# Feed-forward products in two halves of the TensorE array, in a kernel of routed attention and a bilinear feed-forward block

## The chip, the cores and the metric

The kernel runs on one core of a Trainium2 chip. The metric is the time on the device in microseconds, from one launch. Every engine works from a queue of its own: TensorE (PE, matmuls; its weight loads are shown apart as PEld), VectorE (DVE), ScalarE (ACT), GpSimd (POOL) and SyncE (SP), which starts transfers.

## The reference

There are two blocks. The first is attention with routing: queries and keys of each head are assigned to the nearest of 16 centroids, and a query sees only keys of its own cluster. The second is a feed-forward block whose hidden layer is the product of two linear maps. Everything is fp32 outside the kernel.

```python
# q, k, v: (4 batches, 8 heads, 768 tokens, 64); centroids: (8, 16, 64)
q_assign = argmax(q_n @ c_n.T); k_assign = argmax(k_n @ c_n.T)
mask = q_assign[..., :, None] == k_assign[..., None, :]
scores = where(mask, q @ k.T / 8, -1e9)
attn = softmax(scores) @ v                      # (4, 8, 768, 64)
x = attn.transpose(0, 2, 1, 3).reshape(3072, 512)
# w_a, w_b: (512, 1536); w_out: (1536, 512)
out = ((x @ w_a) * (x @ w_b)) @ w_out           # (3072, 512)
```

## The kernel before

The program goes through 96 groups of attention work. In a group, TensorE makes the scores of two tiles of keys (`score`), the weighted values of the two tiles before (`weigh`), sometimes the denominators of the softmax (`denominators`), and then takes feed-forward pieces of an earlier batch from a queue, as many as a budget of matmul columns allows. When the groups are done, the pieces that are left run one after the other.

The scores of two heads of 64 features stand side by side in the rows of the array: each matmul has 64 rows and 128 columns of weights.

```python
def add(Ts, start):                              # in score()
    for u, s in zip(us, tiles):
        p, hf, j = where(u)
        for a in range(2):
            r = slice(a * D, (a + 1) * D)        # D = 64
            nc.tensor.matmul(
                out=s[:, a, 0:HB],               # HB = 384
                lhsT=Ts[p][r, S + j * P:S + (j + 1) * P],
                rhs=Ts[p][r, hf * HB:(hf + 1) * HB],
                start=start, stop=not start)
```

The weighted values of the two heads, and the denominators likewise, stand side by side in its columns: each matmul has 128 rows and 64 columns of weights, and its output is one half of the partitions of a PSUM tile.

```python
for a in range(2):                               # in weigh()
    nc.tensor.matmul(out=O_of[0][a * D:(a + 1) * D, 0:HB],
                     lhsT=vs[p][:, a, j, :], rhs=probs[u][:, a, :],
                     start=(j == 0), stop=(j == NJ - 1))
# ... and in denominators(), for each term t
for a in range(2):
    nc.tensor.matmul(out=ps[a * D:(a + 1) * D, 0:HB], lhsT=ones,
                     rhs=t[:, a, :], ...)
```

The feed-forward products take the whole array, 128 rows and 128 columns of weights. The first batch has the plain form (`up`), the other three split each product of matrices into seven smaller ones in the manner of Strassen (`product`, once for the two maps up, once for the map down; the map down has this form in all batches).

```python
def up(w_sb, f):                                 # 384 columns, 4 in a sum
    ps = ps_m.tile([P, 512], FP32, name="m")
    for ch in range(NCH):
        nc.tensor.matmul(out=ps[:, 0:HB],
                         lhsT=w_sb[:, ch, f * P:(f + 1) * P],
                         rhs=xTs[b][:, ch, t0:t0 + HB],
                         start=(ch == 0), stop=(ch == NCH - 1))
    return ps
# ...
def product(l, r):                               # up: 384 columns, 2 in a sum
    ps = ps_m.tile([P, 512], FP32, name="m")
    rhs = X[r] if r in X else W[r]
    for c in range(2):
        nc.tensor.matmul(out=ps[:, 0:HB], lhsT=A[l][c], rhs=rhs[c],
                         start=(c == 0), stop=(c == 1))
    return ps[:, 0:HB]
# ...
def product(l, r):                               # down: 256 columns, 6 in a sum
    ps = ps_m.tile([P, 512], FP32, name="m")
    for f in range(N2):
        nc.tensor.matmul(out=ps[:, 0:HN], lhsT=A[l][f // 3][:, f % 3, :],
                         rhs=B[r][f // 2][:, f % 2, :],
                         start=(f == 0), stop=(f == N2 - 1))
    return ps[:, 0:HN]
```

VectorE adds a product that is done into one or two tiles in SBUF, and forms the sums and differences of weights and inputs that the next products take. Three PSUM tiles `m` are shared by all these users. The order within one group of the loop:

```python
score(now)
# ...
weigh(before)
ready[l]()               # for some groups: assignments of the next heads (32-column matmuls, L358)
# ...
denominators(*divmod(g // 3 - 1, 2))             # every third group
# ...
while len(ffn) > least and credit > 0:
    cost, piece = ffn.popleft()
    credit -= cost
    piece()
```

Of the kernel before, what the change touches and what calls it, by code (L numbers as in the profile page):

```python
# [30 lines left out]
P = 128  # L31
# [105 lines left out]
def short_path(nc, tc, ctx, c, cn, centroids_in, casts, n_far, q, k, v,  # L137
# [3 lines left out]
    B, H, S, D = q.shape  # L141
# [5 lines left out]
    NCH = DM // P  # L147
    NF = DF // P
    HB = S // 2
# [36 lines left out]
    def by_blocks(p):  # L186
        return p >= HP
# [332 lines left out]
    probs, accs, O_of, den_of, xTs = {}, {}, {}, {}, {}  # L520
# [125 lines left out]

    ffn = deque()

    def store(b, j, half, y):
        order = "(j p) (half n) -> p j half n" if by_blocks(b * HP) else \  # L650
            "(p j) (half n) -> p j half n"
        rows = out[b * S:(b + 1) * S, :].rearrange(order, j=NJ, half=2)
        nc.sync.dma_start(out=rows[:, j, half, :], in_=y)

    def ffn_block(b, blk):

        box = {}
        t0 = blk * HB

        def up(w_sb, f):  # L660
            ps = ps_m.tile([P, 512], FP32, name="m")
            for ch in range(NCH):
                nc.tensor.matmul(out=ps[:, 0:HB],  # L663
                                 lhsT=w_sb[:, ch, f * P:(f + 1) * P],
                                 rhs=xTs[b][:, ch, t0:t0 + HB],
                                 start=(ch == 0), stop=(ch == NCH - 1))
            return ps

        def piece_a(f):
            if f == 0:  # L670
                box["h"] = hp_.tile([P, NF, HB], FP32, name="h")
            ps = up(wa_sb, f)
            box["a"] = hap.tile([P, HB], FP32, name="ha")
            nc.scalar.copy(out=box["a"], in_=ps[:, 0:HB])

        def piece_b(f):
            ps = up(wb_sb, f)
            nc.vector.tensor_tensor(out=box["h"][:, f, :], in0=box["a"],
                                    in1=ps[:, 0:HB], op=ALU.mult)

        ups = [(NCH * HB, lambda f=f, piece=piece: piece(f))
               for f in range(NF) for piece in (piece_a, piece_b)]
        return ups, box
# [41 lines left out]
    def ffn_ups(b, h):  # L725

        x = xTs[b]
        X = {"11": [x[:, c, 0:HB] for c in (0, 1)],
             "T1": [x[:, c, HB:S] for c in (0, 1)],
             "21": [x[:, c, 0:HB] for c in (2, 3)],  # L730
             "22": [x[:, c, HB:S] for c in (2, 3)]}

        def combine_t4():
            for c in range(2):
                nc.vector.tensor_tensor(out=W["T4"][c], in0=W["T2"][c],
                                        in1=X["21"][c], op=ALU.subtract)

        def products(w_sb, i, is_a):
            N2 = NF // 2
            A = {m + n: [w_sb[:, c, f * P:(f + 1) * P] for c in cs]  # L740
                 for m, f in (("1", i), ("2", i + N2))
                 for n, cs in (("1", (0, 1)), ("2", (2, 3)))}
            box = {}

            def combine(name, l, r, op):

                at = {"S1": 1, "S2": 2, "S3": 0, "S4": 3}[name]
                dst = W["slots"][at]
                for c in range(2):
                    nc.vector.tensor_tensor(out=dst[c], in0=l[c], in1=r[c], op=op)  # L750
                A[name] = dst

            def half_1():
                combine("S1", A["21"], A["22"], ALU.add)
                combine("S2", A["S1"], A["11"], ALU.subtract)

            def half_2():
                combine("S3", A["11"], A["21"], ALU.subtract)
                combine("S4", A["12"], A["S2"], ALU.subtract)
                s = W["slots"]  # L760
                W["slots"] = [s[1], s[2], s[0], s[3]]

            def product(l, r):
                ps = ps_m.tile([P, 512], FP32, name="m")
                rhs = X[r] if r in X else W[r]
                for c in range(2):
                    nc.tensor.matmul(out=ps[:, 0:HB], lhsT=A[l][c], rhs=rhs[c],  # L767
                                     start=(c == 0), stop=(c == 1))
                return ps[:, 0:HB]

            def place(k, f):
                if is_a:
                    return h[k][:, f, :]
                return hap.tile([P, HB], FP32, name="ha")

            def add(out, in0, ps, op=ALU.add):
                nc.vector.tensor_tensor(out=out, in0=in0, in1=ps, op=op)  # L777

            def done(name, k, f):
                if not is_a:  # L780
                    to = h[k][:, f, :]
                    nc.gpsimd.tensor_tensor(out=to, in0=to, in1=box[name],  # L782
                                            op=ALU.mult)

            def p1():
                if not h:
                    h.extend(hp_.tile([P, NF, HB], FP32, name="h")
                             for _ in range(2))
                ps = product("11", "11")
                box["11"] = place(0, i)  # L790
                nc.scalar.copy(out=box["11"], in_=ps)

            def p6():
                ps = product("S2", "T2")
                box["12"] = place(1, i)
                add(box["12"], box["11"], ps)

            def p2_ahead():
                box["P2"] = product("12", "21")

            def p2():
                ps = box.pop("P2") if "P2" in box else product("12", "21")
                add(box["11"], box["11"], ps)
                done("11", 0, i)

            def p7():
                ps = product("S3", "T3")
                box["22"] = place(1, i + N2)
                add(box["22"], box["12"], ps)

            def p4():
                ps = product("22", "T4")
                box["21"] = place(0, i + N2)
                add(box["21"], box["22"], ps, ALU.subtract)
                done("21", 0, i + N2)

            def p5():
                ps = product("S1", "T1")
                add(box["12"], box["12"], ps)
                add(box["22"], box["22"], ps)  # L820
                done("22", 1, i + N2)

            def p3():
                add(box["12"], box["12"], product("S4", "22"))
                done("12", 1, i)

            return half_1, half_2, p2_ahead, [p1, p6, p2, p7, p4, p5, p3]

        parts = [products(w_sb, i, w_sb is wa_sb) for i in range(NF // 2)
                 for w_sb in (wa_sb, wb_sb)]  # L830
        pieces = []
        for n, (half_1, half_2, p2_ahead, ps) in enumerate(parts):
            ps[0] = both(*([half_1] if n == 0 else []), half_2, ps[0])
            if n == 0:
                ps[1] = both(p2_ahead, ps[1])
                ps[2] = both(combine_t4, ps[2])
            if n + 1 < len(parts):
                ps[4] = both(ps[4], parts[n + 1][0])
            pieces += [(2 * HB, f) for f in ps]
        return pieces  # L840
# [9 lines left out]
    def ffn_downs(b, h):  # L850
        N2, HN = NF // 2, DM // 2
        B = {m + n: [wo_sb[:, f + i:f + i + 2, c:c + HN] for i in (0, 2, 4)]
             for m, f in (("1", 0), ("2", N2)) for n, c in (("1", 0), ("2", HN))}
# [16 lines left out]
        def tile_of(n):  # L870
            t = slice(n * P, (n + 1) * P)
            A, C = {}, {}
# [17 lines left out]
            def product(l, r):  # L890
                ps = ps_m.tile([P, 512], FP32, name="m")
                for f in range(N2):
                    nc.tensor.matmul(out=ps[:, 0:HN], lhsT=A[l][f // 3][:, f % 3, :],  # L893
                                     rhs=B[r][f // 2][:, f % 2, :],
                                     start=(f == 0), stop=(f == N2 - 1))
                return ps[:, 0:HN]

            def add(out, in0, ps, op=ALU.add):
# [11 lines left out]
            def p2():  # L910
                add(C["11"], C["11"], product("12", "21"))
                store(b, n, 0, C["11"])
                if n == 1:
                    combine("S4", A["12"], "12", "S2")
# [21 lines left out]
            def p4():  # L936
                add(C["21"], C["21"], product("22", "T4"), ALU.subtract)
                store(b, 3 + n, 0, C["21"])
# [27 lines left out]
    def both(*fs):  # L966
        return lambda: [f() for f in fs]
# [72 lines left out]
    for g in range(NG + 3):  # L1040
        p, l = divmod(g, GPP)
# [59 lines left out]
    def some_ffn(n):  # L1101
        for _ in range(n):
# [15 lines left out]
    ps = ps_m.tile([P, 512], FP32, name="m")  # L1118
    nc.tensor.matmul(out=ps[0:1, 0:1], lhsT=far_off, rhs=ones[:, 0:1],
                     start=True, stop=True)  # L1120
# [227 lines left out]
```

## Time and profile before

| | before |
|---|---|
| time, median of 3 runs | 1064.39 us (1064.03 to 1064.41) |
| span of the profiled run | 1062.4 us |
| TensorE busy | 1049.4 us, 4756 matmul records |
| weight loads | 605.4 us |
| VectorE, ScalarE, GpSimd busy | 708.0, 260.0, 354.3 us |
| granted TensorE clock, mean | 0.999 |

A line of a group in the page has the line of the kernel (L767), the engine, the operation, the tiles written and read, the shape of the operands (for a matmul the rows and columns of the weights, then the moving operand), the number of records, then the busy time and the mean of one in ns, and last the idle time of the engine before them with what ended it. L539 are the scores, L580 the weighted values, L603 the denominators, L358 the assignments; L663, L767 and L893 are the three kinds of feed-forward product in the order above. In the timeline the first column is the start in us from the beginning of the span, the second the time from the start of the first to the end of the last of the records that were merged. One fp32 matmul of the program appears as two records; records of TensorE overlap one another.

### The profile page before, as it was taken

To read this page: it belongs to the slowest core of one execution; us is meant where nothing else is said; L and a number is where in the kernel's file an instruction comes from. 1 tells how busy PE (TensorE), PEld (TensorE's weight loads), DVE (VectorE), ACT (ScalarE), POOL (GpSimd) and SP (SyncE) were. 2 spreads that over 40 slices of the span, in tenths; PEclk is the share of its full clock that TensorE was granted. 3 is DMA by queue.
4 is the path that set the end of the run, shared out by engine and by line. 5 is a ranking of instruction groups with operands and counts; after the bars stand their busy time and mean duration, and the time that the engine had idled before them with its cause. 6 is when DMAs were issued, how large, how long until landed. Compare 5 with 4: busy or idle time off the path is not lost.

```text
span 1062.4 us, 13065 instructions
## 1 busy us (share of the span) xinstructions
PE 1049.4 (99%) x4756; PEld 605.4 (57%) x4756; DVE 708.0 (67%) x1402; ACT 260.0 (24%) x501; POOL 354.3 (33%) x329
## 2 busy tenths in 40 slices
PE   8999999999999999999999999999999999999997
PEld 5444455554557665455445766555545687555686
DVE  6778877887857447676757736767565846676762
ACT  5665333233322221222222121122121200000000
POOL 1111345454533322443545422444334310222200
PEclk9999999999999999999999999999999999999999
DMA  6334253525130120202020030200000000000001
GB/s 173 92 71 99 84 105 104 124 76 131 62 47 20 39 41 22 38 4 45 5 45 1 25 65 24 46 0 20 0 4 1 11 30 21 0 1 1 0 31 33
DMA packets 120504, 46.18 MB, mean 43 GB/s; under 512 B 106608, under 2 KB 115824, under 8 KB 120432
## 3 DMA queue, kind: packets, MB, share of 16 engines
q1 hardware_dynamic: 120016, 44.85, 18.1%
q8 instruction: 39, 0.64, 0.3%
q10 hardware_dynamic: 416, 0.43, 0.1%
q14 instruction: 33, 0.27, 0.1%
HBM read 37.78 MB, written 6.29 MB: 41 GB/s over the span
## 4 chain that ended last, share of the span: by engine, by line
PE 93%; DVE 5%; issue 1%; POOL 1%; DMA 0%; ACT 0%; DVEq 0%; POOLq 0%
PE m L767 30%; PE m L893 20%; PE s L539 14%; PE O L580 12%; PE m L663 11%; PE m L603 2%; PE m L358 1%; DVE raw L723 1%; PE m L342 0%; DVE raw L750 0%; DVE acc L569 0%; DVE xT L723 0%; POOL xT L635 0%; DVE ha L777 0%; DMA wo_sb<-in_centroids_dram 0%
## 5 line engine op out<-in xcount | busy, mean ns | idle before, releaser
L548 ACT ACTIVATE pt<-s 128x768 f32<-128x768 f32 x192 | 145.4, 808 | 307.4 <-PE s L539 253.8
L569 POOL TENSOR_TENSOR acc<-acc,pt 128x384 f32<-128x384 f32 x144 | 151.9, 1068 | 59.8 <-ACT pt L548 43.5
L782 POOL TENSOR_TENSOR h<-h,ha 128x384 f32<-128x384 f32 x72 | 72.6, 1016 | 235.9 <-DVE ha L777 234.4
L580 PE MATMUL O<-pt,v 128*64 128x384 f32 x768 | 145.1, 499 | 0.0
L539 PE MATMUL s<-qkT 64*128 64x384 f32 x768 | 139.6, 483 | 0.0
L777 DVE TENSOR_TENSOR ha<-ha,m 128x384 f32<-128x384 f32 x126 | 66.9, 546 | 74.1 <-PE m L767 73.3
L777 DVE TENSOR_TENSOR h<-h,m 128x384 f32<-128x384 f32 x126 | 67.3, 549 | 64.3 <-PE m L767 63.5
L569 DVE TENSOR_TENSOR acc<-acc,pt 128x384 f32<-128x384 f32 x96 | 73.7, 794 | 35.9 <-POOL acc L569 35.0
L580 PEld LDWEIGHTS O<-pt,v 128*64 128x64 f32 x768 | 46.6, 136 | 86.4 <-issue 84.8
L539 PEld LDWEIGHTS s<-qkT 64*128 64x128 f32 x768 | 70.5, 187 | 31.4 <-issue 0.2
L893 PE MATMUL m<-wo_sb,h 128*128 128x256 f32 x384 | 87.5, 382 | 0.0
L635 POOL TENSOR_TENSOR xT<-xT,acc 128x384 f32<-128x384 f32 x32 | 32.9, 1029 | 147.9 <-DVE acc L630 121.3
L893 PEld LDWEIGHTS m<-wo_sb,h 128*128 128x128 f32 x384 | 72.1, 190 | 16.0 <-issue 4.2
L767 PE MATMUL m<-raw 128*128 128x384 f32 x192 | 70.4, 489 | 0.9 <-DVE ha L777 0.9
L663 PE MATMUL m<-xT,wa_sb 128*128 128x384 f32 x192 | 67.4, 493 | 0.7 <-POOL xT L635 0.7
L663 PE MATMUL m<-xT,wb_sb 128*128 128x384 f32 x192 | 66.8, 491 | 0.0
L893 PE MATMUL m<-xT,h 128*128 128x256 f32 x288 | 65.4, 382 | 0.1
L893 PEld LDWEIGHTS m<-xT,h 128*128 128x128 f32 x288 | 54.1, 190 | 11.7 <-issue 1.7
L767 PE MATMUL m<-xT,wa_sb 128*128 128x384 f32 x144 | 52.9, 491 | 0.4 <-DVE rest L899 0.4
L767 PE MATMUL m<-xT,size 128*128 128x384 f32 x144 | 52.8, 490 | 0.0
L767 PE MATMUL m<-xT,wb_sb 128*128 128x384 f32 x144 | 52.8, 490 | 0.0
L663 PEld LDWEIGHTS m<-xT,wa_sb 128*128 128x128 f32 x192 | 35.4, 190 | 30.5 <-ACT pt L548 3.6
(164 smaller groups left out, 1444.6 us busy)
## 6 DMA issues: line engine op xcount, KB each, us to landing
raw<-in_moe_w_a_dram SPq DMA_DIRECT2D x12, 512.0 KB, 4.4
raw<-in_moe_w_b_dram SPq DMA_DIRECT2D x12, 512.0 KB, 3.7
raw<-in_moe_w_out_dram SPq DMA_DIRECT2D x12, 512.0 KB, 3.3
qk<-in_q_dram SPq DMA_DIRECT2D x48, 96.0 KB, 3.1
qk<-in_k_dram SPq DMA_DIRECT2D x48, 96.0 KB, 3.6
v<-in_v_dram SPq DMA_DIRECT2D x24, 192.0 KB, 3.9
out_dram<-rest SPq DMA_DIRECT2D x24, 128.0 KB, 1.7
v<-in_v_dram SPq DMA_DIRECT2D x4, 384.0 KB, 4.6
```

What stands on the lines that cost most here:

```text
L358: nc.tensor.matmul(out=ps[32 * kq:32 * kq + 32, 0:HB], lhsT=cTb[:, hp, :], rhs=qkTs[p][:, kq * HB:(kq + 1) * HB], start=True, stop=True)
L539: nc.tensor.matmul(out=s[:, a, 0:HB], lhsT=Ts[p][r, S + j * P:S + (j + 1) * P], rhs=Ts[p][r, hf * HB:(hf + 1) * HB], start=start, stop=not ...
L548: nc.scalar.activation(out=pt, in_=s[:, :, 0:HB], func=AF.Exp, scale=SCALE)
L569: eng.tensor_tensor(out=acc[:, a, :], in0=probs[u - 1][:, a, :] if j == 1 else acc[:, a, :], in1=probs[u][:, a, :], op=ALU.add)
L580: nc.tensor.matmul(out=O_of[0][a * D:(a + 1) * D, 0:HB], lhsT=vs[p][:, a, j, :], rhs=probs[u][:, a, :], start=(j == 0), stop=(j == NJ - 1))
L603: nc.tensor.matmul(out=ps[a * D:(a + 1) * D, 0:HB], lhsT=ones, rhs=t[:, a, :], start=(n == 0), stop=(n == len(terms) - 1))
L635: nc.gpsimd.tensor_tensor(out=x, in0=x, in1=den, op=ALU.mult)
L663: nc.tensor.matmul(out=ps[:, 0:HB], lhsT=w_sb[:, ch, f * P:(f + 1) * P], rhs=xTs[b][:, ch, t0:t0 + HB], start=(ch == 0), stop=(ch == NCH - 1))
L767: nc.tensor.matmul(out=ps[:, 0:HB], lhsT=A[l][c], rhs=rhs[c], start=(c == 0), stop=(c == 1))
L777: nc.vector.tensor_tensor(out=out, in0=in0, in1=ps, op=op)
L782: nc.gpsimd.tensor_tensor(out=to, in0=to, in1=box[name], op=ALU.mult)
L893: nc.tensor.matmul(out=ps[:, 0:HN], lhsT=A[l][f // 3][:, f % 3, :], rhs=B[r][f // 2][:, f % 2, :], start=(f == 0), stop=(f == N2 - 1))
```

## The change

Each feed-forward product is made of two matmuls with 64 columns of weights, one in each half of the array's columns, with the same moving operand; their outputs are the two halves of the partitions of the same PSUM tile. The scores, the weighted values, the denominators and all work of the other engines stay as they are. It is meant to give the products the same division of the array as the weighted values and the denominators, which run just before them in a group, so that the array need not change its division between the two.

```diff
+    def in_halves(ps, lhsT, rhs, start, stop):
+        for a in range(2):
+            half = slice(a * D, (a + 1) * D)
+            nc.tensor.matmul(out=ps[half], lhsT=lhsT[:, half], rhs=rhs,
+                             start=start, stop=stop)
 # ... in up()
-                nc.tensor.matmul(out=ps[:, 0:HB],
-                                 lhsT=w_sb[:, ch, f * P:(f + 1) * P],
-                                 rhs=xTs[b][:, ch, t0:t0 + HB],
-                                 start=(ch == 0), stop=(ch == NCH - 1))
+                in_halves(ps[:, 0:HB], w_sb[:, ch, f * P:(f + 1) * P],
+                          xTs[b][:, ch, t0:t0 + HB],
+                          start=(ch == 0), stop=(ch == NCH - 1))
 # ... in product(), up
-                    nc.tensor.matmul(out=ps[:, 0:HB], lhsT=A[l][c], rhs=rhs[c],
-                                     start=(c == 0), stop=(c == 1))
+                    in_halves(ps[:, 0:HB], A[l][c], rhs[c],
+                              start=(c == 0), stop=(c == 1))
 # ... in product(), down
-                    nc.tensor.matmul(out=ps[:, 0:HN], lhsT=A[l][f // 3][:, f % 3, :],
-                                     rhs=B[r][f // 2][:, f % 2, :],
-                                     start=(f == 0), stop=(f == N2 - 1))
+                    in_halves(ps[:, 0:HN], A[l][f // 3][:, f % 3, :],
+                              B[r][f // 2][:, f % 2, :],
+                              start=(f == 0), stop=(f == N2 - 1))
```

## The prediction

> **What bounds the kernel now.** I read the page first, for the engine that sets the end.
>
> ```profile
> PE 1049.4 (99%) x4756; PEld 605.4 (57%) x4756; DVE 708.0 (67%) x1402; ACT 260.0 (24%) x501; POOL 354.3 (33%) x329
> ...
> PE 93%; DVE 5%; issue 1%; POOL 1%; DMA 0%; ACT 0%; DVEq 0%; POOLq 0%
> ...
> L580 PE MATMUL O<-pt,v 128*64 128x384 f32 x768 | 145.1, 499 | 0.0
> L580 PEld LDWEIGHTS O<-pt,v 128*64 128x64 f32 x768 | 46.6, 136 | 86.4 <-issue 84.8
> L893 PE MATMUL m<-wo_sb,h 128*128 128x256 f32 x384 | 87.5, 382 | 0.0
> L893 PEld LDWEIGHTS m<-wo_sb,h 128*128 128x128 f32 x384 | 72.1, 190 | 16.0 <-issue 4.2
> L767 PE MATMUL m<-raw 128*128 128x384 f32 x192 | 70.4, 489 | 0.9 <-DVE ha L777 0.9
> ```
>
> TensorE is busy 1049.4 of 1062.4 us and makes 93% of the chain of work that ended last. In the chain the feed-forward lines L767, L893 and L663 hold 30%, 20% and 11%, the scores (L539) 14%, the weighted values (L580) 12%. The mean of one matmul is no cost here, because matmuls overlap: 768 records of L580 at 499 ns fill 145.1 us only. (Every fp32 matmul of the program is two records; counts below are records.) What a matmul costs is the distance from its start to the next start, so I read the timeline of TensorE over two of the groups of work that repeat through most of the run: scores, weighted values, then feed-forward products.
>
> ```profile
> 499.64 0.81 PE L539 MATMUL s<-qkT 64*128 64x384 f32 x4
> 500.38 1.51 PE L580 MATMUL O<-pt,v 128*64 128x384 f32 x8
> 501.82 1.56 PE L767 MATMUL m<-xT,size 128*128 128x384 f32 x4
> 503.21 1.45 PE L767 MATMUL m<-xT,wb_sb 128*128 128x384 f32 x4
> 504.50 1.45 PE L767 MATMUL m<-raw 128*128 128x384 f32 x4
> 505.79 1.45 PE L767 MATMUL m<-xT,wb_sb 128*128 128x384 f32 x4
> 507.08 1.45 PE L767 MATMUL m<-raw 128*128 128x384 f32 x4
> 508.47 0.50 PE L539 MATMUL s<-ohT 64*128 64x384 bf16 x4
> 508.80 1.45 PE L539 MATMUL s<-qkT 64*128 64x384 f32 x8
> 510.19 1.51 PE L580 MATMUL O<-pt,v 128*64 128x384 f32 x8
> ```
>
> The first column is the start. Between the starts of steady products (503.21, 504.50, 505.79, 507.08) lie 1.29 us for four full-width matmuls: 0.322 us each. The eight half-width records of O are four pairs, so their streaming is also 4 x 0.322 = 1.29 us, but 500.38 to 501.82 is 1.44 us: 0.15 more. The first product after O takes 501.82 to 503.21 = 1.39 us, 0.10 more. And 507.08 to 508.47 (products to scores) and 508.80 to 510.19 (scores to O) are each 1.39, again 0.10 more. So there is no wait on another engine in these stretches; what is lost is lost wherever the shape of the array changes. Going through every start of the trace, the median excess over streaming is: scores to O 0.094 us, then 0.051 at the second pair of O; O to product 0.100, then 0.104 at the second matmul of the product; product to scores 0.096, then 0.010. Inside a run of one shape it is 0.000, for the 64-column pairs (gap 0.323) as for full-width matmuls (0.323 at 384 columns, 0.216 at 256).
>
> Last, whether others would keep up: the busy time by stretch (columns: TensorE, weight loads, VectorE, ScalarE, GpSimd, clock), and who waits for whom.
>
> ```profile
> 410.00:570.00 160.00, 159.56 (x664) 80.64 (x662) 104.85 (x221) 34.18 (x66) 65.77 (x64) 1.00 0.14 25
> 575.00:655.00 80.00, 80.00 (x410) 56.75 (x410) 50.12 (x89) 15.79 (x34) 33.81 (x25) 1.00 0.15 34
> 900.00:1000.00 100.00, 100.00 (x312) 58.90 (x311) 68.79 (x166) 5.26 (x11) 21.36 (x22) 1.00 0.00 0
> ```
>
> ```profile
> POOL h L782 <- DVE ha L777: 234.4, 54, 25.5
> DVE ha L777 <- PE m L767: 73.3, 75, 4.2
> ```
>
> VectorE is busy two thirds of each stretch and stands waiting for TensorE 75 times at the products; the clock is full. The stretch at 900 us is one long run of products without attention.
>
> **What the Trainium skill says.** "TensorEngine Tiling (Array Packing)", Key Properties, says that changing the tiling mode, not just the tile, drains TensorE, and Tiling Modes lists two tiles of 128x64 as a mode of its own. The trace agrees: 0.10 us at each change of shape and nothing between the halves of one shape. "TensorE: Matmul & The Clock Gate", Measured speedup vs the span model, gives a packed group the time of one matmul plus about 4 ns per further tile; the trace shows halves starting 7 ns apart (500.375 and 500.382) and no loss in the sustained gap. The same page, LDWEIGHTS (loading the stationary operand), gives a load a time that goes with its columns, columns / 1.2 in ns: from 128 to 64 columns that is an estimate of 53 ns less, and the trace has 190 and 136 ns, 54 less.
>
> **The change, part by part.** *Removed:* the change of shape between O (or the denominators, L603, which use the same two halves) and the products. I counted the entries into products in the start times: 49 come directly from O (13 to L663, 23 to L767, 13 to L893) and 25 from the denominators (7, 10, 8), together 74. Each loses its 0.100 and its 0.104 us, since pair after pair of one shape has excess 0.000: 74 x 0.204 = 15.1 us. After the last scores, products also go back straight to O once and to the denominators once, at 855 and 865 us; those lose 0.093 + 0.051 each, 2 x 0.144 = 0.3 us. One entry from the four-quarter matmul of L358 stays a change, but loads 64 columns: 0.05 us. At about six places products wait for VectorE inside their run, and their second matmul then shows the 0.104 of an unhidden full-width load; half-width shows 0.051: 6 x 0.05 = 0.3 us.
>
> *Added:* 2400 records of products (384 of L663, 1008 of L767, 1008 of L893) become 4800, with as many loads. A pair streams in the time of one, so 0 us for them, in 384 columns by measurement and in 256 columns by inference: the two loads start 7 ns apart, at 137 ns each they end after 0.144 us, under the 0.216 us of a 256-column pair. A product's last half ends 7 ns later; VectorE has slack for this. *Unchanged in kind:* products to scores remains a change; the change from halves to scores shows 0.102 in the five direct ones of O against 0.096 from full width: 72 x 0.006 = 0.4 us more. Scores to O stays 0.094 + 0.051.
>
> *Moved:* the order of pieces on every engine is the same, because pieces are dealt out by columns, which do not change. TensorE gets to the waits that do exist about 0.2 us earlier per group. Idle or late starts inside products sum to some 4 us now (0.84 at 114, 0.37 at 403, 0.61 at 517, 0.36 at 657, 0.61 at 770, 0.27 at 1009 us). Where VectorE or GpSimd has a backlog over a group or two, TensorE's saving of 0.2 to 0.4 us is given back as a longer wait: five places in the attention part, about 0.25 us each, 1.2 us. No gain lies before 112 us (no products yet) nor after 866 us (some 190 us of products alone).
>
> Sum: -15.1 - 0.3 - 0.05 - 0.3 + 0.4 + 1.2 = -14.1 us, so 1064.4 - 14.1 = 1050.3 us, 1.3% less.
>
> **The rivals.** *Issue or load becomes the bound in the 256-column products.* Four instructions must be issued every 0.216 us, sustained for up to 216 records; now there are two. For it: nothing in this trace sustains such a rate. Against: the four bf16 records of the scores run as two pairs 0.17 us apart with four instructions each, and at 310 us the quarters of L358 start four loads and four matmuls in 20 ns. If a pair took 0.24 instead of 0.216, 1008 x 0.025 = 25 us would be added: about 1075 us, slower by 1%. *Two halves that read the same columns disturb each other.* In O the halves read different right-hand sides, in the change the same one at the same time. If so every pair is longer; doubled, it would be 2400 x about 0.28 = 670 us. Against: the two streams of O read the same partitions of one tile at full speed and the four streams of L358 do so too. *The saving turns into waits.* If VectorE, which has 35% of free time but works in bursts, ended each group, half of the 15 us would go: 1057 us. Against: the idle time of products in the page is under 1 us a row, and VectorE waits for TensorE, not the other way.
>
> **Range and chances.** The size per change is a median with almost no spread, and the count is exact, so the main term is sure to a microsecond. What is open is the give-back (0.5 to 7 us) and the two rivals that lengthen pairs, perhaps one chance in fifteen together. Range 1047.5 to 1056. Over 2% faster would take 21 us, more than all the changes of shape removed are worth: 0.02. Over 2% slower needs a rival: 0.04. Within 2%: 0.94.
>
> **What would show it.** In the timeline of a group like that at 500 us: O to product 1.34 us for O's four pairs (0.05 left), the first product 1.29 us, as all others; scores to O still 1.39. In the groups, product lines at twice the count and loads of about 137 ns. In the stretch of products alone at the end, starts of pairs 0.216 and 0.322 us apart as now: longer gaps there mean the issue or read rival. Idle time before products in front of VectorE or GpSimd above 2 to 3 us in the sum means the give-back. The prediction is wrong if pairs stream slower than single matmuls, or if entering products from O still costs 0.1 us.

## The result and the profile after

| | before | after |
|---|---|---|
| time, median of 5 runs | 1064.41 us (1064.03 to 1064.46) | 1052.06 us (1051.98 to 1052.57) |
| span of the profiled run | 1062.4 us | 1050.6 us |
| TensorE busy, matmul records | 1049.4 us, 4756 | 1036.5 us, 7156 |
| weight loads | 605.4 us | 510.6 us |

The ratio is 0.9886, with a 95% interval of 0.9873 to 0.9900: 12.35 us less. The lines of the page that answer to those of before:

```profile
PE 1036.5 (99%) x7156; PEld 510.6 (49%) x7156; DVE 709.6 (68%) x1402; ACT 260.6 (25%) x501; POOL 355.7 (34%) x329
...
PE 92%; DVE 5%; issue 1%; POOL 1%; ACT 0%; DMA 0%; DVEq 0%; POOLq 0%
...
L654 PE MATMUL m<-xT,wa_sb 128*64 128x384 f32 x672 | 119.3, 487 | 1.7 <-POOL xT L635 0.9
L654 PE MATMUL m<-wo_sb,h 128*64 128x256 f32 x768 | 86.7, 379 | 0.0
...
L654 PEld LDWEIGHTS m<-xT,wa_sb 128*64 128x64 f32 x672 | 49.2, 137 | 61.3 <-issue 50.6
```

TensorE is still the engine that sets the end. 768 half records of the group m<-wo_sb,h fill 86.7 us, where 384 whole ones filled 87.5: twice the records, the same time. A load of 64 columns takes 137 ns, where one of 128 took 190. The saving is seen in the timeline of TensorE over the same group as the one shown of before (first column the start):

```profile
495.16 1.51 PE L580 MATMUL O<-pt,v 128*64 128x384 f32 x8
496.50 1.46 PE L654 MATMUL m<-xT,size 128*64 128x384 f32 x8
497.79 1.46 PE L654 MATMUL m<-xT,wb_sb 128*64 128x384 f32 x8
499.08 1.46 PE L654 MATMUL m<-raw 128*64 128x384 f32 x8
500.37 1.46 PE L654 MATMUL m<-xT,wb_sb 128*64 128x384 f32 x8
501.66 1.46 PE L654 MATMUL m<-raw 128*64 128x384 f32 x8
503.06 0.50 PE L539 MATMUL s<-ohT 64*128 64x384 bf16 x4
503.39 1.45 PE L539 MATMUL s<-qkT 64*128 64x384 f32 x8
504.77 1.51 PE L580 MATMUL O<-pt,v 128*64 128x384 f32 x8
```

O to the first product is 1.34 us (1.44 before) and the first product takes 1.29 us (1.39 before), like all others. Products to scores (501.66 to 503.06) is 1.40 us (1.39 before), scores to O (503.39 to 504.77) 1.38 (1.39 before). From O to the next O it is 9.61 us, 9.81 before: 0.20 us a group. Where products run alone the pace stayed. Two stretches of the changed kernel after the last group, then the second of them in the kernel before, by the view of busy time by stretch (the stretch, its length, then TensorE's busy time with its records, then the weight loads):

```profile
888.00:988.00 100.00, 100.00 (x622) 44.55 (x620) 68.93 (x166) 5.27 (x11) 21.41 (x22) 1.00 0.00 1
998.00:1043.00 45.00, 45.00 (x420) 35.99 (x418) 20.88 (x47) 1.29 (x4) 0.00 (x0) 1.00 0.09 31
```

```profile
1010.00:1055.00 45.00, 45.00 (x210) 39.46 (x209) 20.80 (x46) 1.29 (x4) 0.00 (x0) 1.00 0.10 31
```

622 half records in 100 us are 311 pairs, where there were 312 whole records before. In the second stretch, at 256 columns, 420 halves make 210 pairs in 45 us, where there were 210 whole records.

Laying the starts of all scores of the two traces beside each other gives the saving group by group (groups are named by the time at which they ended before). Of the 72 groups with products, 59 save 0.196 to 0.199 us. But three go the other way: 0.25 us are lost in the group that ends at 200 us, 0.83 us in the one at 259 us, and 0.20 us in the one at 592 us. The first two have the assignments L358 and lie in the stretch in which VectorE rounds the weights; the third is taken up further down. At the second of them, TensorE before and after:

```profile
250.28 1.51 PE L580 MATMUL O<-pt,v 128*64 128x384 f32 x8
251.72 0.85 PE L358 MATMUL m<-qkT,cTb 128*32 128x384 f32 x8
252.50 0.87 PE L603 MATMUL m<-acc,ones 128*64 128x384 f32 x4
```

```profile
248.69 1.51 PE L580 MATMUL O<-pt,v 128*64 128x384 f32 x8
250.31 1.70 PE L358 MATMUL m<-qkT,cTb 128*32 128x384 f32 x8
251.94 0.87 PE L603 MATMUL m<-acc,ones 128*64 128x384 f32 x4
```

and VectorE's two transposes that make the input of L358, before and after:

```profile
249.83 1.83 DVE L460 STREAM_TRANSPOSE qkT<-qk 128x768 f32<-128x768 f32 x2
```

```profile
249.29 1.83 DVE L460 STREAM_TRANSPOSE qkT<-qk 128x768 f32<-128x768 f32 x2
```

Before, the second transpose ended at 251.66 and L358 started at 251.72: the transpose was just in time, and no wait showed. After, TensorE starts O 1.6 us sooner, but VectorE is only 0.54 us ahead of before. L358 starts with the first transpose (ended 250.26), stops for the second (251.12), and its eight records take 1.70 us instead of 0.85.

### The profile page after: what moved, and what is told of

Read it like the earlier page. It is cut to its first block, busy times and chain, and to the rows that moved or that the text cites. A ratio compares the mean times of both kernels' runs of the same rounds, so it can differ in the third digit from the quotient of the medians.

```text
span 1050.6 us, 17937 instructions
## 1 busy us (share of the span) xinstructions
PE 1036.5 (99%) x7156; PEld 510.6 (49%) x7156; DVE 709.6 (68%) x1402; ACT 260.6 (25%) x501; POOL 355.7 (34%) x329
## 4 chain that ended last, share of the span: by engine, by line
PE 92%; DVE 5%; issue 1%; POOL 1%; ACT 0%; DMA 0%; DVEq 0%; POOLq 0%
PE m L654 61%; PE s L539 14%; PE O L580 12%; PE m L603 2%; PE m L358 1%; DVE raw L730 1%; PE m L342 1%; POOL xT L635 1%; DVE raw L757 0%; DVE xT L730 0%; DVE raw L874 0%; DVE ha L784 0%; DVE acc L630 0%; DVE acc L569 0%; DVE acc L623 0%
## 5 line engine op out<-in xcount | busy, mean ns | idle before, releaser
L654 PE MATMUL m<-xT,wa_sb 128*64 128x384 f32 x672 | 119.3, 487 | 1.7 <-POOL xT L635 0.9
L654 PE MATMUL m<-xT,wb_sb 128*64 128x384 f32 x672 | 119.1, 486 | 0.0
L654 PE MATMUL m<-wo_sb,h 128*64 128x256 f32 x768 | 86.7, 379 | 0.0
L654 PEld LDWEIGHTS m<-xT,wa_sb 128*64 128x64 f32 x672 | 49.2, 137 | 61.3 <-issue 50.6
L654 PEld LDWEIGHTS m<-xT,wb_sb 128*64 128x64 f32 x672 | 49.2, 137 | 59.3 <-issue 55.4
L654 PE MATMUL m<-raw 128*64 128x384 f32 x384 | 70.2, 486 | 1.1 <-DVE ha L784 1.1
L654 PEld LDWEIGHTS m<-wo_sb,h 128*64 128x64 f32 x768 | 57.3, 137 | 28.3 <-issue 3.9
L654 PE MATMUL m<-xT,h 128*64 128x256 f32 x576 | 64.8, 379 | 0.1
L654 PE MATMUL m<-xT,size 128*64 128x384 f32 x288 | 52.6, 486 | 0.0
L539 PE MATMUL s<-ohT 64*128 64x384 bf16 x384 | 48.1, 328 | 0.5 <-DVE ohT L441 0.5
```

The costliest lines, as they stand in the source:

```text
L539: nc.tensor.matmul(out=s[:, a, 0:HB], lhsT=Ts[p][r, S + j * P:S + (j + 1) * P], rhs=Ts[p][r, hf * HB:(hf + 1) * HB], start=start, stop=not ...
L654: nc.tensor.matmul(out=ps[half], lhsT=lhsT[:, half], rhs=rhs, start=start, stop=stop)
```

## The experiments

**One: the halves in the first piece only.** The first piece of each group is in halves, all others use the whole array.

```diff
+    whole = [True]
 # ... in in_halves()
+        if whole[0]:
+            nc.tensor.matmul(out=ps, lhsT=lhsT, rhs=rhs, start=start, stop=stop)
+            return
         for a in range(2):
 # ... in the loop over groups
+            whole[0] = False
             while len(ffn) > least and credit > 0:
                 cost, piece = ffn.popleft()
                 credit -= cost
                 piece()
+                whole[0] = True
 # ... after the last group
+    whole[0] = True
```

> Only the first piece of each group's feed-forward work is in halves, all other products use the whole array. Theory A (the gain is the changes of the array's division that are no longer made between O or the denominators and the products): the change is only moved by one piece, each of the 74 entries costs its 0.10 + 0.10 us again one product later, so the time is that of the kernel before, 1064.4 us, within 0.7 us (ratio 1.000). Theory B (loads of 64 columns are shorter and leave TensorE sooner): about one product in five is in halves, so about a fifth of the 12.35 us remains, some 2.5 us: 1062 us. Theory C (only the first product after O matters, whatever follows it): the full gain, 1052 us.

Measured: 1064.67 us against 1064.77 us for the kernel before, measured with it, ratio 1.000 (0.9991 to 1.0009). The timeline of TensorE in this kernel:

```profile
500.62 1.51 PE L580 MATMUL O<-pt,v 128*64 128x384 f32 x8
501.96 1.46 PE L658 MATMUL m<-xT,size 128*64 128x384 f32 x8
503.35 1.56 PE L654 MATMUL m<-xT,wb_sb 128*128 128x384 f32 x4
504.74 1.45 PE L654 MATMUL m<-raw 128*128 128x384 f32 x4
...
510.43 0.54 PE L580 MATMUL O<-pt,v 128*64 128x384 f32 x2
```

O to the half product is 1.34 us, without the 0.10; half to whole is 1.39 and the first whole product 1.39: both amounts come back one product later, and O to O is 9.81 us as before. Half the array's columns as such bring nothing, and going in without a change brings nothing if the change follows. Theory A holds; B (2.5 us less, ratio 0.998) and C (1052 us) lie outside the interval.

**Two: the whole array after attention.** Halves in the loop, whole products in what is left.

```diff
+    whole = [False]
 # ... in_halves() as in the first experiment; after the last group
+    whole[0] = True
 
     def some_ffn(n):
         for _ in range(n):
             ffn.popleft()[1]()
```

> Halves while attention runs, the whole array for the products that are left after the last group (about 190 us of products alone). Theory A: there are no changes of division in that stretch to save, one is added at its start, so the time is that of the changed kernel plus 0.2 us: 1052.3 us, ratio 0.9887. Theory B (the gain is in the products themselves): the share of the products that are left alone, about a quarter, is lost: 1055 us.

Measured: 1052.84 us, ratio 0.9887 (0.9870 to 0.9903); the span is 0.23 us longer than that of the changed kernel. The products that run alone have no part in the gain; theory B's 1055 us would be a ratio of 0.991, outside the interval.

**Three: quarters.** 32 columns of weights, four matmuls a product.

```diff
-        for a in range(2):
-            half = slice(a * D, (a + 1) * D)
-            nc.tensor.matmul(out=ps[half], lhsT=lhsT[:, half], rhs=rhs,
+        for a in range(4):
+            part = slice(a * 32, (a + 1) * 32)
+            nc.tensor.matmul(out=ps[part], lhsT=lhsT[:, part], rhs=rhs,
                              start=start, stop=stop)
```

> All products as four matmuls of 32 weight columns in the quarters of the array. Theory A: O (two halves) to products (four quarters) is a change of division again. From the trace before, O to the four quarters of L358 loses 0.100 us and the second set of quarters 0.024 us, and quarters to scores 0.116 against 0.102 us: 74 x 0.124 + 72 x 0.014 = 10.2 us over the changed kernel, 1062.3 us, ratio 0.998. Theory B (shorter loads): at or under 1052 us. Rival D (issue becomes the bound): eight instructions per 0.216 us in the 256-column products; if they were issued one per 0.035 us, each set of quarters would take 0.28 us, 1008 x 0.065 = 65 us more.

Measured: 1061.22 us, ratio 0.9965 (0.9953 to 0.9978). The timeline of TensorE:

```profile
500.09 1.51 PE L580 MATMUL O<-pt,v 128*64 128x384 f32 x8
501.53 1.50 PE L654 MATMUL m<-xT,size 128*32 128x384 f32 x16
502.85 1.47 PE L654 MATMUL m<-xT,wb_sb 128*32 128x384 f32 x16
504.14 1.47 PE L654 MATMUL m<-raw 128*32 128x384 f32 x16
```

O to quarters is 1.44 us again, the first product 1.32, the next 1.29. Group by group this kernel loses 0.137 or 0.138 us against the changed one; the expectation was 0.124 + 0.014. It came out about 1 us below 1062.3 because most of the waits at 200 and 259 us are gone when TensorE comes later again: those two groups gain 0.31 and 0.41 us on the changed kernel instead of losing 0.14. The loads got shorter still (110 ns against 137) and the kernel slower, so theory B falls:

```profile
L654 PEld LDWEIGHTS m<-wo_sb,h 128*32 128x32 f32 x1536 | 50.9, 110 | 35.9 <-issue 4.5 <-PE O L580 1.8 <-DVE xT L874 0.6
```

Rival D falls too: in the 256-column products the median distance of two sets of quarters is 0.216 us, with eight instructions in each.

**Four: VectorE transposes before it rounds.** The changed kernel, with VectorE's order turned round in the groups that have both.

```diff
+        while parts and l == 0 and todo:
+            todo.popleft()()
         round_next()
```

> The changed kernel with one edit for VectorE alone: in the groups in which the queries and keys of the next heads are transposed and weights are rounded, VectorE transposes first and rounds after. In the trace of the changed kernel TensorE's assignments (L358) at 192 and 250 us start with half their inputs and wait for the second transpose, and about 0.45 and 1.03 us of the saving are gone there. Theory A (the give-back is VectorE's order in these groups, and VectorE has slack later): both come back, 1.5 us less than the changed kernel, 1050.6 us, ratio 0.987. Theory B (VectorE bounds that stretch whatever its order): the same wait appears at the next product or acc, and the time stays 1052.1 us.

Measured: 1052.40 us, ratio 0.9888 (0.9873 to 0.9903): no gain over the changed kernel. The first of the two groups has its 0.45 us back, but at the second another 0.49 us is lost, and 0.58 us more in a later group (at 294 us of this kernel), whose scores wait for the transfer of the one-hot rows. TensorE at the second group of this kernel, then VectorE:

```profile
247.57 1.51 PE L580 MATMUL O<-pt,v 128*64 128x384 f32 x8
249.01 0.85 PE L358 MATMUL m<-qkT,cTb 128*32 128x384 f32 x8
251.32 0.87 PE L603 MATMUL m<-acc,ones 128*64 128x384 f32 x4 [1.46 <-DVE h L685]
```

```profile
246.75 1.82 DVE L460 STREAM_TRANSPOSE qkT<-qk 128x768 f32<-128x768 f32 x2
...
250.72 0.55 DVE L685 TENSOR_TENSOR h<-ha,m 128x384 f32<-128x384 f32 x1
```

L358 no longer waits, but the transposes and the rest of the rounding now stand ahead of the product that VectorE takes out of PSUM (L685), which started at 248.83 us in the changed kernel and starts at 250.72 here. L603 needs its tile and waits 1.46 us. Theory A holds at the first group alone. At the second it was not the order of the two that cost: VectorE is behind at this place of the group, and the wait goes to the next one that needs something of it.

**Five: the assignments at the end of the group.** The changed kernel, with L358 of 11 pairs of heads, and VectorE's transpose of its result, after the group's products.

```diff
-        return [[lambda: across(0), lambda: across(1)], [sims_across],
+        sim_steps[p] = sims_across
+        return [[lambda: across(0), lambda: across(1)], [],
 # ... in prep_steps()
-            ready[1] = both(lambda: prep_sim(p), lambda: load_v(p), ready[1])
+            if p == HP:
+                ready[1] = both(lambda: prep_sim(p), lambda: load_v(p), ready[1])
+            else:
+                ready[1] = lambda: load_v(p)
 # ... at the end of the group
+        if l == 1 and p + 1 in sim_steps:
+            prep_sim(p + 1)
+            sim_steps[p + 1]()
```

> The changed kernel with the four-quarter assignments of the next heads moved, for the 11 pairs of heads after the fifth, from between O and the products to the end of the group, between the products and the next scores, and VectorE's transpose of their result with them. Theory A (each change of division costs what the trace shows): O to quarters 0.100 + 0.024 and quarters to halves 0.114 + 0.05 us fall away, products to quarters 0.100 + 0.024 and quarters to scores 0.116 take the place of products to scores 0.102: 0.15 us less each, 1.65 us; and TensorE no longer waits for the transposes at 192 and 250 us, 1.5 us: 3.1 us less than the changed kernel, 1049.0 us, ratio 0.9855. Rival (what TensorE saves is spent waiting for VectorE, GpSimd or a PSUM tile): 1051 to 1052 us.

Measured: 1048.50 us, ratio 0.9845 (0.9832 to 0.9859), the fastest of all: 3.9 us less than the fourth, measured with it, and 1.5% below the kernel before. TensorE in the group that had the second wait (the lines of this kernel's scores, O and denominators are L545, L586 and L609):

```profile
247.32 1.51 PE L586 MATMUL O<-pt,v 128*64 128x384 f32 x8
248.66 0.81 PE L609 MATMUL m<-acc,ones 128*64 128x384 f32 x4
249.31 2.75 PE L660 MATMUL m<-xT,wb_sb 128*64 128x384 f32 x16
251.89 2.75 PE L660 MATMUL m<-xT,wa_sb 128*64 128x384 f32 x16
254.57 0.85 PE L358 MATMUL m<-qkT,cTb 128*32 128x384 f32 x8
255.35 0.50 PE L545 MATMUL s<-ohT 64*128 64x384 bf16 x4
```

O, denominators and products follow one another without a change, and the quarters stand at the end, where a change was made anyhow: two changes take the place of three. Seven of the 11 groups save 0.151 us against the changed kernel. The two at 200 and 259 us save 0.598 and 1.181, which is 0.151 and the 0.447 and 1.030 that were lost there. The last two (436 and 690 us) save 0.293: one of their products, which still started 0.09 us late in the changed kernel, no longer does. The sum of these steps is 3.43 us where 3.1 was expected. So VectorE did have room: later in the same group, with the transposes due after the products and not before them.

## Why the prediction was right

The time fell into the range, 1.8 us above the predicted 1050.3. In the profiled runs the gain is 11.9 us, 2.2 less than the 14.1 of the sum.

- *What is lost at changes of shape, and 74 entries at 0.204 us.* Right. The groups show 0.197 to 0.198, which is 0.204 less the 0.006 that halves to scores costs more, as the prediction had it. The first experiment shows that the change itself is the cost, the third that another change of shape in the same place costs what the trace said it would.
- *Pairs of 256 columns at no cost.* Right: 0.216 us before and after, and still with quarters. This was inferred; now it is measured. Both rivals that lengthen pairs are gone, including the one of two halves that read the same columns.
- *No gain before 112 us and after 866 us.* Right; the second experiment shows it for the products alone.
- *The give-back, 1.2 us in five places.* The mechanism was right, the term was too small. Summed over the groups that saved less than 0.197 us it is about 2.7 us, so this term carries 1.5 of the 2.2 us. The five places that the prediction named gave back only 0.63 (0.15 at 121, 0.18 at 406 and at 660, 0.06 at 519 and at 773 us), and 0.2 went in small pieces. What was missed are three waits: the two of L358 for VectorE's transposes, 0.45 and 1.03 us, which the fifth experiment, with L358 later, has back, and one of 0.39 us in the group at 592 us, where products take differences of the output weights that VectorE forms (lines below). They were missed because the prediction looked at waits that existed. A hand-over that ends 0.06 us before it is needed shows no wait at all; and since VectorE does not follow TensorE in this stretch, TensorE did not come 0.2 us early, as one group's saving, but by the sum of the groups since 112 us, less what had been given back.
- *Shorter loads where products wait, 0.3 us.* Not seen as a saving of its own: no group saves more than 0.199 us, so where products wait it only lowered what was given back, and it is already in the 2.7.
- Of the rest, 0.4 us lie ahead of all feed-forward work: the first scores start at 11.2 us instead of 10.8. In the profiled runs of the seven kernels this start lies anywhere between 10.5 and 12.2 us, with nothing changed there, so I take no meaning from it.

The group at 592 us, before and after, VectorE's three differences and the products that take them:

```profile
587.12 3.65 DVE L867 TENSOR_TENSOR raw<-wo_sb 128x512 f32<-128x512 f32 x3
...
589.17 2.78 PE L893 MATMUL m<-raw,ha 128*128 128x256 f32 x12
```

```profile
580.31 3.97 DVE L874 TENSOR_TENSOR raw<-wo_sb 128x512 f32<-128x512 f32 x3
...
582.24 1.90 PE L654 MATMUL m<-raw,ha 128*64 128x256 f32 x16
584.33 1.08 PE L654 MATMUL m<-raw,ha 128*64 128x256 f32 x8 [0.20 <-DVE raw L874]
```

Before, the last difference ended at 590.77 us and the first record that takes it started at 590.90, in step with the record ahead of it. After, the products start 6.9 us sooner and the last difference ends only 6.5 us sooner, at 584.28, so they stop for it. No experiment took this wait away.

## What to carry to other kernels

Look at the distance between matmul starts, not at busy time: this TensorE, at 99%, lost 0.1 to 0.2 us at every change of the array's division. Giving neighbours in the queue the same division, or moving a piece with its own division to where a change is made anyhow, took that back here at no cost in streaming. When the bounding engine gets faster by a little in every group, the little adds up against each engine that does not depend on it; look for hand-overs that are in time by less than the whole saving up to that place, not by less than one group's. And moving such a producer ahead on its own engine moves the wait to the next consumer; moving the consumer later can remove it.

## What the runs showed of the hardware

- A change has two parts. The first is about 0.10 us whichever shapes meet (medians of 0.093 to 0.116 us in these traces). The second is seen at the second matmul: 0.104 us with 128 columns of weights, 0.051 with 64, 0.024 with 32, all fp32; the bf16 matmuls that open the scores show at most 0.010. The second part also follows a wait without a change of shape: before, a product that had waited started at 403.70 us and the next matmul at 404.13, 0.104 us over the 0.323 of streaming. So I read it as a first load that is not hidden, and the drain that "TensorEngine Tiling (Array Packing)", Key Properties, speaks of as the first part only; no experiment separates the two.
- Four quarters of the array keep the rate of one whole matmul with eight instructions in 0.216 us, one per 27 ns, over whole products. The prediction had held the issue for a risk at half of that rate.
